# Attention and ReGLU on one core: block 2's scores, values and output copies rearranged amid six output units

## The chip, the cores and the metric

The kernel runs on one core of one Trainium2 chip. The metric is the device time of one execution in microseconds (us). The engines of the core are TensorE (PE: matmuls, with weight loads shown apart as PEld), VectorE (DVE), ScalarE (ACT), GpSimd (POOL) and SyncE (SP). SyncE, ScalarE and GpSimd also issue DMA transfers; in the profile these issues are named SPq, ACTq and POOLq, or appear as DMA_DIRECT2D and DMA_TRANSPOSE.

## The reference

Chunked attention with 8 memory rows in front, then a feed-forward layer with a ReLU gate. Shapes: q, k, v (4, 8, 768, 64), memories (4, 8, 8, 64), gate and value weights (512, 1536), output weights (1536, 512); the output is (3072, 512) in float32.

```python
for c in range(768 // 32):                       # chunks of 32 queries
    c0, c1 = 32 * c, 32 * c + 32
    l0, r1 = max(0, c0 - 16), min(768, c1 + 8)   # keys: 16 to the left, 8 to the right
    k_full = concat([mem_k, k[:, :, l0:r1]], axis=2)
    v_full = concat([mem_v, v[:, :, l0:r1]], axis=2)
    scores = matmul(q[:, :, c0:c1], k_full.T) / 8
    a = exp(scores - max(scores))
    a = a / (sum(a) + 1e-9)
    attn[:, :, c0:c1] = matmul(a, v_full)
x = attn.transpose(0, 2, 1, 3).reshape(3072, 512)
out = (maximum(x @ w_gate, 0) * (x @ w_val)) @ w_out
```

## The kernel before, in words

The 3072 tokens are cut into 8 blocks of 384 (`TB`); a block is half a batch row with all 8 heads. Heads are handled in 4 pairs (`HP`). A block's 384 queries are four windows (`NQ`) of 96, and each window has 128 keys (8 memory rows and a band of 120).

A block's work has two halves. **Attention**, per head pair: `step_s` makes the scores (4 matmuls into `sc_ps`, which has one buffer) and three exponentials on ScalarE (`ex`); `step_v` multiplies `ex` with the values (8 matmuls into `xo_ps` and `xs_ps`, one bank each, whose upper 64 rows are the sums) and takes the logarithm of the sums (`ln`); `step_e` exponentiates to get the reciprocal (`rinv`); `step_m` multiplies both on VectorE into `xT`. **Feed-forward**, in 15 units: 12 gate/value units (`ffn_unit`: 4 gate and 4 value matmuls into two banks, ReLU on ScalarE, product on VectorE) and 3 output units (`out_unit`: 12 matmuls of 512 columns into one bank, copied to `o_sb`, stored). The banks of `g_ps`, `v_ps` and `o_ps` come from one pool of four (`bank`).

The order is written out by hand, and each engine runs its own instructions in that order. Blocks 0 and 1 are opened by a list of steps (`go`). Then `run` weaves the attention of block n into the units of the block ahead of it: `at` says after which unit a head pair's scores come, and `off` how many units later its values come. For block 2 the units are the 12 gate/value units of block 1 and then six output units, three of block 0 and three of block 1. Scores of the four head pairs come after output units 2, 3, 4 and 5, and values half a unit later, in the middle of the next output unit.

From block 2 on, keys and queries reach their layout in four steps: GpSimd's queue loads them (`load_band`, `load_q_tokens`, within `loads`), SyncE issues two DMA transposes (`turn_dma`: `kT`, then `qT`), GpSimd copies the queries apart for the two heads of each pair (`spread_q`, into `qbd`), and TensorE makes the scores. GpSimd runs these in program order: the spread of block 2, the loads of block 3, the spread of block 3, the loads of block 4, and so on.

Of the kernel before, what the change touches and what calls it, by code (L numbers as in the profile page):

```python
# [8 lines left out]
F32 = mybir.dt.float32  # L9
F16 = mybir.dt.float16  # L10
# [7 lines left out]
def kernel(  # L18
# [12 lines left out]
    nc = tc.nc  # L31
# [60 lines left out]
    filler = const.tile([128, 512], F16, name="filler")  # L92
    xo, xs = (xps.tile([128, 512], F32, name=nm)[:, 0:TB] for nm in ("xo_ps", "xs_ps"))
    bias16 = const.tile([128, 3], F16, name="bias16")
    bias1 = const.tile([128, 3], F32, name="bias1")
    perm = const.tile([128, 128], F16, name="perm")
    mln64 = const.tile([128, 1], F32, name="mln64")
    wg = const.tile([128, NFC, DFF], F16, name="wg")
# [130 lines left out]

    def turn_dma(n):  # L230
        kTs[n] = turned.tile([128, NQ, HP, 128], F16, tag="kT", name="kT")
        qTs[n] = turned.tile([128, NQ, HP, QB], F16, tag="qT", name="qT")
        nc.sync.dma_start_transpose(kTs[n].rearrange("p i a m -> p (i a) m"),  # L233
                                    k16s[n % 2].rearrange("p i h d -> p (i h d)"))
        nc.sync.dma_start_transpose(qTs[n].rearrange("p i a m -> p (i a) m"),
                                    q16s[n].rearrange("p i h d -> p (i h d)"))

    def spread_q(n):

        for hh in range(2):  # L240
            s = slice(D * hh, D * hh + D)
            nc.gpsimd.tensor_copy(qbds[n % 2][s, :, :, hh, :].rearrange("p i a m -> p (i a) m"),  # L242
                                  qTs[n][s].rearrange("p i a m -> p (i a) m"))

# [87 lines left out]
    def step_v(n, hp):  # L332
        ex, vw = exs.pop((n, hp)), vwins[n % 2]
        for i in range(NQ):
            for hh in range(2):
                nc.tensor.matmul((xo, xs)[hh][:, QB * i:QB * i + QB], lhsT=vw[:, i, 2 * hp + hh, :],  # L336
                                 rhs=ex[:, hh, i, :], start=True, stop=True)
        ln = rpool.tile([D, 2, TB], F32, name="ln")
        for hh in range(2):
            nc.scalar.activation(ln[:, hh], (xo, xs)[hh][D:128], ACT.Ln, scale=1.0 / 64.0)  # L340
        lns[n, hp] = ln
# [6 lines left out]
    def step_m(n, hp):  # L348
        rinv = rinvs.pop((n, hp))
        for hh in range(2):  # L350
            nc.vector.tensor_tensor(out=x_of(n)[D * hh:D * hh + D, hp, :], in0=(xo, xs)[hh][0:D],  # L351
                                    in1=rinv[:, hh, :], op=ALU.mult)
# [48 lines left out]
    def out_unit(n, t, between=()):  # L401
# [10 lines left out]
        if last:  # L412
            for s, copy, dma in ((slice(0, 256), dve_copy, sp), (slice(256, 512), act_copy, act_dma)):
                copy(o_sb[:, s], o_ps[:, s])
                dma(out[row0:row0 + 128, s], o_sb[:, s])
        else:
            nc.scalar.copy(o_sb, o_ps)  # L417
            act_dma(out[row0:row0 + 128, :], o_sb)
# [226 lines left out]
    load_mem_v(2)  # L645
    turn_dma(2)
    load_band(2, v, vwins)
# [17 lines left out]


    STEP = {"s": step_s, "v": step_v, "e": step_e, "m": step_m}

    def pieces(n, what):
        for w, hp in what:  # L670
            STEP[w](n, hp)

    def run(order, n, at, off, turn_at):
        for u, (b, x) in enumerate(order):
            now = [hp for hp in range(HP) if n < NB and u == at[hp] + off]
            if n < NB:
                pieces(n, [("m", hp) for hp in range(HP) if u == at[hp] + off + 1])
            inner, outer = ("ve", "") if x >= NDC else ("v", "e")  # L680
            unit(b, x, [lambda w=(w, hp): pieces(n, [w]) for hp in now for w in inner])
# [3 lines left out]
            if n == 2 and u < len(clear):  # L685
                clear[u]()
            if u == turn_at and n + 1 < NB:
                turn_dma(n + 1)
                spread_q(n + 1)
        if n < NB:  # L690
            pieces(n, [("m", hp) for hp in range(HP) if len(order) == at[hp] + off + 1])

# [44 lines left out]
```

## Time and profile before

| | us |
|---|---|
| median of 3 runs (lowest, highest) | 245.21 (240.61, 245.4) |
| profiled execution, its own time | 241.14 |
| its span, first to last instruction | 239.1 |

The table of the page in 40 slices of 5.98 us each; each digit is the busy share in tenths:

```profile
PE   7899999999876599999999999999999999999994
DVE  4677548871031245512662155604652166314400
ACT  3473874432577488927984589728892699434321
POOL 8879655623980696199059602990040000000000
PEclk9999999999999999999999999999999999999999
DMA  6999999999999699979959999799901100120012
```

The stretch around the change is slices 9 to 14 (54 to 84 us). In the rows that follow, "idle before" and the square brackets give the idle time of the engine ahead of an instruction and what ended it. Line numbers are those of the kernel before.

### The profile page before, as it was taken

What the parts mean: (1) busy time and instruction counts of PE and PEld (TensorE: products, weight loads), DVE (VectorE), ACT (ScalarE), POOL (GpSimd) and SP (SyncE); (2) the same over time, 40 slices, a digit from 0 to 9 for tenths busy, and PEclk for the clock granted to TensorE, in tenths of its full rate; (3) what the DMA queues carried; (4) which work ended last, traced back from release to release, by engine and by line L of the source; (5) the groups of instructions that cost most, each with busy time, mean ns of one, the idle gap of its engine ahead of it and who ended that gap; (6) DMA issues with size and microseconds to landing.
All of it is one profiled execution on the core that took longest, in us unless ns stands there. A gap on an engine that the chain in (4) does not pass through costs nothing.

```text
span 239.1 us, 4590 instructions
## 1 busy us (share of the span) xinstructions
PE 225.6 (94%) x1727; PEld 130.8 (55%) x1727; DVE 104.8 (44%) x204; ACT 142.7 (60%) x300; POOL 104.2 (44%) x131
## 2 busy tenths in 40 slices
PE   7899999999876599999999999999999999999994
PEld 3556455655433266646664566546664666555541
DVE  4677548871031245512662155604652166314400
ACT  3473874432577488927984589728892699434321
POOL 8879655623980696199059602990040000000000
PEclk9999999999999999999999999999999999999999
DMA  6999999999999699979959999799901100120012
GB/s 164 175 195 196 196 192 206 154 129 128 136 174 185 161 100 151 142 88 187 164 87 90 183 151 102 50 171 132 169 3 61 71 3 0 44 91 0 1 44 88
DMA packets 110143, 28.47 MB, mean 119 GB/s; under 512 B 93882, under 2 KB 107178, under 8 KB 110122
## 3 DMA queue, kind: packets, MB, share of 16 engines
q0 software_dynamic: 81760, 15.13, 79.6%
q1 hardware_dynamic: 24490, 6.50, 19.0%
q10 hardware_dynamic: 3872, 6.56, 8.3%
q8 instruction: 13, 0.21, 0.4%
q14 instruction: 8, 0.07, 0.1%
HBM read 31.08 MB, written 6.29 MB: 156 GB/s over the span
## 4 chain that ended last, share of the span: by engine, by line
PE 67%; DMA 19%; POOL 7%; SPq 2%; issue 2%; DVE 1%; ACT 0%
PE g_ps L372 20%; PE v_ps L372 20%; PE o_ps L408 18%; DMA qT<-q16n 5%; DMA wg<-in_moe_w_gate_dram 5%; DMA k<-in_k_dram 4%; PE sc_ps L279 3%; DMA vwin<-in_v_dram 2%; POOL k L145 2%; SPq L233 2%; POOL qbd L242 2%; DMA kst<-in_k_dram 2%; PE xo_ps L336 1%; PE xs_ps L336 1%; POOL q16n L171 1%
## 5 line engine op out<-in xcount | busy, mean ns | idle before, releaser
L384 DVE TENSOR_TENSOR gv<-v_ps,gr 128x384 f16<-128x384 f32 x95 | 52.5, 555 | 88.7 <-ACT gr L380 72.8
L372 PE MATMUL g_ps<-xT,wg 128*128 128x384 f16 x380 | 78.5, 326 | 1.3 <-DVE xT L351 1.3
L372 PE MATMUL v_ps<-xT,wv 128*128 128x384 f16 x380 | 78.1, 326 | 0.4 <-DMA wv<-in_moe_w_val_dram 0.4
L408 PE MATMUL o_ps<-wo,gv 128*128 128x512 f16 x288 | 64.6, 379 | 0.0
L380 ACT ACTIVATE gr<-g_ps 128x384 f16<-128x384 f32 x95 | 46.3, 488 | 26.1 <-PE g_ps L372 13.5
L372 PEld LDWEIGHTS <-wv 128*128 128x128 f16 x384 | 36.1, 98 | 24.1 <-issue 1.5
L372 PEld LDWEIGHTS <-wg 128*128 128x128 f16 x384 | 36.7, 98 | 22.8 <-issue 0.2
L408 PEld LDWEIGHTS <-gv 128*128 128x128 f16 x288 | 27.9, 98 | 31.3
L242 POOL COPY qbd<-qT 64x1536 f16<-64x1536 f16 x12 | 17.6, 1464 | 58.8 <-DMA qT<-q16n 58.4
L291 ACT ACTIVATE ex<-sc_ps,bias 128x256 f16<-128x256 f32 x84 | 33.4, 469 | 6.8 <-PE sc_ps L255 2.4
L417 ACT COPY o_sb<-o_ps 128x512 f32<-128x512 f32 x23 | 13.5, 586 | 35.1 <-PE o_ps L408 24.9
L351 DVE TENSOR_TENSOR xT<-xo_ps,rinv 64x384 f16<-64x384 f32 x24 | 13.2, 550 | 25.1 <-ACT rinv L345 25.1
L145 POOL DMA_DIRECT2D k<-in_k_dram x24 | 21.5, 905 | 2.9 <-DMA wv<-in_moe_w_val_dram 1.9
L345 ACT ACTIVATE rinv<-ln,mln 64x768 f32<-64x768 f32 x24 | 22.2, 925 | 0.1
L145 POOL DMA_DIRECT2D vwin<-in_v_dram x24 | 21.8, 940 | 0.4 <-PE v_ps L372 0.4
L171 POOL DMA_DIRECT2D q16n<-in_q_dram x24 | 18.7, 798 | 3.4 <-DMA wo<-in_moe_w_out_dram 3.4
L340 ACT ACTIVATE ln<-xo_ps 64x384 f32<-64x384 f32 x24 | 11.7, 487 | 13.7 <-PE xs_ps L336 13.7
L336 PEld LDWEIGHTS <-vwin 128*128 128x128 f16 x192 | 10.9, 98 | 8.6 <-issue 5.5
L336 PE MATMUL xo_ps<-ex,vwin 128*128 128x96 f16 x96 | 11.2, 206 | 4.3 <-ACT ex L291 4.3
L351 DVE TENSOR_TENSOR xT<-xs_ps,rinv 64x384 f16<-64x384 f32 x24 | 13.2, 551 | 0.7
L279 PE MATMUL sc_ps<-qbd,kT 128*128 128x192 f16 x96 | 11.8, 246 | 1.3 <-POOL qbd L242 1.3
L340 ACT ACTIVATE ln<-xs_ps 64x384 f32<-64x384 f32 x24 | 11.4, 474 | 0.0
(89 smaller groups left out, 128.4 us busy)
## 6 DMA issues: line engine op xcount, KB each, us to landing
out_dram<-o_sb ACTq DMA_DIRECT2D x23, 256.0 KB
q16n<-in_q_dram POOLq DMA_DIRECT2D x24, 96.0 KB, 5.3
k<-in_k_dram POOLq DMA_DIRECT2D x18, 120.0 KB, 4.8
vwin<-in_v_dram POOLq DMA_DIRECT2D x18, 120.0 KB, 7.6
wg<-in_moe_w_gate_dram POOLq DMA_DIRECT2D x6, 256.0 KB, 8.4
wv<-in_moe_w_val_dram POOLq DMA_DIRECT2D x6, 256.0 KB, 8.7
wo<-in_moe_w_out_dram POOLq DMA_DIRECT2D x3, 512.0 KB, 11.6
rv<-in_v_dram POOLq DMA_DIRECT2D x4, 224.0 KB, 8.1
```

What stands on the lines that cost most here:

```text
L145: pool_dma(dsts[p][NMEM + m0:NMEM + m1, i, :, 0:D], src)
L171: pool_dma(q16s[n][:, i], src)
L242: nc.gpsimd.tensor_copy(qbds[n % 2][s, :, :, hh, :].rearrange("p i a m -> p (i a) m"), qTs[n][s].rearrange("p i a m -> p (i a) m"))
L291: nc.scalar.activation(flat[:, :, :, s], view[:, :, :, s], ACT.Exp, scale=SCALE, bias=(bias1 if n == 1 else bias)[:, g:g + 1])
L336: nc.tensor.matmul((xo, xs)[hh][:, QB * i:QB * i + QB], lhsT=vw[:, i, 2 * hp + hh, :], rhs=ex[:, hh, i, :], start=True, stop=True)
L340: nc.scalar.activation(ln[:, hh], (xo, xs)[hh][D:128], ACT.Ln, scale=1.0 / 64.0)
L345: nc.scalar.activation(rinv, lns.pop((n, hp)), ACT.Exp, scale=-1.0, bias=mln64[0:D, :])
L351: nc.vector.tensor_tensor(out=x_of(n)[D * hh:D * hh + D, hp, :], in0=(xo, xs)[hh][0:D], in1=rinv[:, hh, :], op=ALU.mult)
L372: nc.tensor.matmul(ps[a], lhsT=(wg, wv)[a][:, f, 128 * m:128 * m + 128], rhs=xTs[n][:, f, :], start=(f == 0), stop=(f == NFC - 1))
L380: nc.scalar.activation(grs[n, m], g_ps, ACT.Relu)
L384: nc.vector.tensor_tensor(out=gvs[n][:, m, :], in0=v_ps, in1=grs.pop((n, m)), op=ALU.mult)
L408: nc.tensor.matmul(o_ps, lhsT=gvs[n][:, m, 128 * t:128 * t + 128], rhs=wo[:, m, :], start=(m == 0), stop=(m == NDC - 1))
```

## The change

Between block 1's gate/value units and block 2's own units, and at the start of block 2's units, the order becomes another one:

- `run1` and `pair2` replace the general `run` for block 2. Scores and exponentials of head pair hp come in the middle of output unit hp+2, and its values one unit later, directly behind the next pair's scores.
- Values of pairs 0 and 2 go to two banks of the pool of four (`xo2_ps`, `xs2_ps`), those of pairs 1 and 3 to `xo_ps` and `xs_ps`.
- `spread_q(2)` runs on VectorE. Every spread is now four copies, the first head pair's two ahead. On GpSimd a copy of one column (`gate`) from `kT` of block 2 stands ahead of the loads of block 3, where the spread stood.
- The six output units are copied by VectorE and stored by SyncE; `o_sb` has 4 buffers in place of 3. The transposes of block 3 come at output units 2 (`kT`) and 3 (`qT`), in program order between these stores, where both stood at unit 4 before.
- Block 2's first two gate/value units are computed together, chunk by chunk (`chunk`), and block 3's scores come after units 1, 4, 7 and 10 in place of 0, 3, 6 and 9.

The diff, cut to its core:

```diff
-    opool = ctx.enter_context(tc.tile_pool(name="opool", bufs=3))
+    opool = ctx.enter_context(tc.tile_pool(name="opool", bufs=4))
...
-    def spread_q(n):
-        for hh in range(2):
-            s = slice(D * hh, D * hh + D)
-            nc.gpsimd.tensor_copy(qbds[n % 2][s, :, :, hh, :].rearrange("p i a m -> p (i a) m"),
-                                  qTs[n][s].rearrange("p i a m -> p (i a) m"))
+    def spread_q(n, copy=nc.gpsimd.tensor_copy):
+        for a in (slice(0, 1), slice(1, HP)):
+            for hh in range(2):
+                s = slice(D * hh, D * hh + D)
+                copy(qbds[n % 2][s, :, a, hh, :], qTs[n][s, :, a, :])
...
     def step_v(n, hp):
         ex, vw = exs.pop((n, hp)), vwins[n % 2]
+        if n == 2 and hp % 2 == 0:
+            xo, xs = (bank(nm)[:, 0:TB] for nm in ("xo2_ps", "xs2_ps"))
+        else:
+            xo, xs = xo_ps, xs_ps
+        vbanks[n, hp] = xo, xs
...
+        elif n < 2:
+            dve_copy(o_sb, o_ps)
+            sp(out[row0:row0 + 128, :], o_sb)
         else:
             nc.scalar.copy(o_sb, o_ps)
             act_dma(out[row0:row0 + 128, :], o_sb)
...
+            if n == 3 and u < 2:
+                if u == 0:
+                    ffn_open(2, (0, 1))
+                    for f in range(NFC):
+                        chunk(2, f)
+                    ffn_close(2)
+            else:
+                unit(n - 1, u, ...)
...
+    def pair2(hp):
+        if hp < HP:
+            score(2, hp)
+        if hp > 0:
+            step_v(2, hp - 1)
+        if hp > 1:
+            step_m(2, hp - 2)
+        if hp < HP:
+            score_exp(2, hp)
+        if hp > 0:
+            step_ln(2, hp - 1)
+            step_e(2, hp - 1)
+
+    def run1():
+        for u in range(NDC):
+            unit(1, u)
+            if u < len(clear):
+                clear[u]()
+        spread_q(2, dve_copy)
+        for t in range(2 * NT):
+            out_unit(t // NT, t % NT, [lambda: pair2(t - 1)] if t > 0 else [])
+            if t == 1:
+                turn_k_dma(3)
+            if t == 2:
+                turn_q_dma(3)
+            if t == 3:
+                spread_q(3)
+        step_m(2, HP - 1)
...
-    spread_q(2)
+    nc.gpsimd.tensor_copy(gate, kTs[2][:, NQ - 1, HP - 1, 0:1])
     loads(3)
-    run([(1, m) for m in range(NDC)] + [(b, NDC + t) for b in range(2) for t in range(NT)], 2, (13, 14, 15, 16), 1, 15)
+    run1()
     for n in range(2, NB):
         loads(n + 2)
-        run([(n, u) for u in range(NDC + NT)], n + 1, (0, 3, 6, 9), 2, 9)
+        run(n + 1, (1, 4, 7, 10) if n == 2 else (0, 3, 6, 9))
```

Three places show how the change moves instructions. ScalarE first, at the output units, in the kernel before (numbers tell buffers apart; `ex` with `x3` are a head pair's exponentials):

```order
L417 COPY o_sb_1085<-o_ps_1072 128x512
L418 DMA out_0_dram<-o_sb_1085 128x512
L417 COPY o_sb_1101<-o_ps_1088 128x512
L418 DMA out_0_dram<-o_sb_1101 128x512
L291 ACTIVATE ex_1109<-sc_ps_1104,bias_103 128x8x32 x3
L340 ACTIVATE ln_1128<-xo_ps_107 64x384
L340 ACTIVATE ln_1128<-xs_ps_108 64x384
L345 ACTIVATE rinv_1131<-ln_1128,mln64_112 64x768
L417 COPY o_sb_1139<-o_ps_1113 128x512
L418 DMA out_0_dram<-o_sb_1139 128x512
L291 ACTIVATE ex_1147<-sc_ps_1142,bias_103 128x8x32 x3
L340 ACTIVATE ln_1169<-xo_ps_107 64x384
```

And in the changed kernel:

```order
L294 ACTIVATE ex_1104<-sc_ps_1099,bias_103 128x8x32 x3
L294 ACTIVATE ex_1141<-sc_ps_1126,bias_103 128x8x32 x3
L350 ACTIVATE ln_1145<-xo2_ps_1131 64x384
L350 ACTIVATE ln_1145<-xs2_ps_1132 64x384
L355 ACTIVATE rinv_1148<-ln_1145,mln64_113 64x768
L294 ACTIVATE ex_1184<-sc_ps_1168,bias_103 128x8x32 x3
L350 ACTIVATE ln_1188<-xo_ps_107 64x384
L350 ACTIVATE ln_1188<-xs_ps_108 64x384
L355 ACTIVATE rinv_1191<-ln_1188,mln64_113 64x768
```

The copies and stores of the output units are gone from between the steps, and the exponentials of pair 1 stand ahead of pair 0's logarithms.

GpSimd, from the spread of block 2 (`qbd0_96`) to the spread of block 3 (`qbd1_97`), before:

```order
L242 COPY qbd0_96<-qT_578 64x16x96 x2
L145 DMA k161_93<-in_k_dram 120x8x64 x3
L145 DMA k161_93<-in_k_dram 112x8x64
L171 DMA q16n_892<-in_q_dram 96x8x64 x4
L145 DMA vwin1_95<-in_v_dram 120x8x64 x3
L145 DMA vwin1_95<-in_v_dram 112x8x64
L242 COPY qbd1_97<-qT_1193 64x16x96 x2
```

And in the changed kernel:

```order
L752 COPY gate_112<-kT_578 128x1
L146 DMA k161_93<-in_k_dram 120x8x64 x3
L146 DMA k161_93<-in_k_dram 112x8x64
L172 DMA q16n_892<-in_q_dram 96x8x64 x4
L146 DMA vwin1_95<-in_v_dram 120x8x64 x3
L146 DMA vwin1_95<-in_v_dram 112x8x64
L246 COPY qbd1_97<-qT_1159 64x4x96 x2
L246 COPY qbd1_97<-qT_1159 64x4x3x96 x2
```

The two copies of `qT` ahead of block 3's loads have become one copy of a column of `kT`.

SyncE's queue, from the memory rows of block 3 (`k161_93`, `vwin1_95`) to those of block 4 (`k160_92`, `vwin0_94`), before:

```order
L156 DMA k161_93<-memk_98 8x4x512
L161 DMA vwin1_95<-memv_99 8x8x64 x4
L233 DMA_TRANSPOSE kT_1192<-k161_93 128x16x128
L235 DMA_TRANSPOSE qT_1193<-q16n_892 128x16x96
L156 DMA k160_92<-memk_98 8x4x512
L161 DMA vwin0_94<-memv_99 8x8x64 x4
```

And in the changed kernel:

```order
L157 DMA k161_93<-memk_98 8x4x512
L162 DMA vwin1_95<-memv_99 8x8x64 x4
L428 DMA out_0_dram<-o_sb_1089 128x512
L428 DMA out_0_dram<-o_sb_1114 128x512
L233 DMA_TRANSPOSE kT_1117<-k161_93 128x16x128
L428 DMA out_0_dram<-o_sb_1156 128x512
L238 DMA_TRANSPOSE qT_1159<-q16n_892 128x16x96
L428 DMA out_0_dram<-o_sb_1199 128x512
L428 DMA out_0_dram<-o_sb_1245 128x512
L428 DMA out_0_dram<-o_sb_1276 128x512
L157 DMA k160_92<-memk_98 8x4x512
L162 DMA vwin0_94<-memv_99 8x8x64 x4
```

Two output stores now precede the K transpose of block 3, one stands between the two transposes, and three follow.

More of the change, by code (lines that the diff above doesn't have):

```diff
@@ L92 @@
     filler = const.tile([128, 512], F16, name="filler")
-    xo, xs = (xps.tile([128, 512], F32, name=nm)[:, 0:TB] for nm in ("xo_ps", "xs_ps"))
+    xo, xs = xo_ps, xs_ps = [xps.tile([128, 512], F32, name=nm)[:, 0:TB] for nm in ("xo_ps", "xs_ps")]
     bias16 = const.tile([128, 3], F16, name="bias16")
@@ L96 @@
     perm = const.tile([128, 128], F16, name="perm")
+    gate = const.tile([128, 1], F16, name="gate")
     mln64 = const.tile([128, 1], F32, name="mln64")
@@ L337, in step_v, with step_ln @@
                                  rhs=ex[:, hh, i, :], start=True, stop=True)
+    def step_ln(n, hp):
         ln = rpool.tile([D, 2, TB], F32, name="ln")
         for hh in range(2):
-            nc.scalar.activation(ln[:, hh], (xo, xs)[hh][D:128], ACT.Ln, scale=1.0 / 64.0)
+            nc.scalar.activation(ln[:, hh], vbanks[n, hp][hh][D:128], ACT.Ln, scale=1.0 / 64.0)
         lns[n, hp] = ln
@@ L350, in step_m @@
         for hh in range(2):
-            nc.vector.tensor_tensor(out=x_of(n)[D * hh:D * hh + D, hp, :], in0=(xo, xs)[hh][0:D],
+            nc.vector.tensor_tensor(out=x_of(n)[D * hh:D * hh + D, hp, :], in0=vbanks[n, hp][hh][0:D],
                                     in1=rinv[:, hh, :], op=ALU.mult)
@@ L645 @@
     load_mem_v(2)
-    turn_dma(2)
+    turn_k_dma(2)
+    turn_q_dma(2)
     load_band(2, v, vwins)
@@ L671, in pieces, with run @@
             STEP[w](n, hp)
-    def run(order, n, at, off, turn_at):
-        for u, (b, x) in enumerate(order):
-            now = [hp for hp in range(HP) if n < NB and u == at[hp] + off]
+    def run(n, at):
+        for u in range(NDC + NT):
             if n < NB:
-                pieces(n, [("m", hp) for hp in range(HP) if u == at[hp] + off + 1])
-            inner, outer = ("ve", "") if x >= NDC else ("v", "e")
-            unit(b, x, [lambda w=(w, hp): pieces(n, [w]) for hp in now for w in inner])
+                pieces(n, [("m", hp) for hp in range(HP) if u == at[hp] + 3])
+            now = [hp for hp in range(HP) if n < NB and u == at[hp] + 2]
+            inner, outer = ("ve", "") if u >= NDC else ("v", "e")
+            if n == 3 and u < 2:
[5 more added lines that the diff above has]
+            else:
+                unit(n - 1, u, [lambda w=(w, hp): pieces(n, [w]) for hp in now for w in inner])
             pieces(n, [(w, hp) for hp in now for w in outer])
@@ L684, in run @@
                 pieces(n, [("s", hp) for hp in range(HP) if u == at[hp]])
-            if n == 2 and u < len(clear):
-                clear[u]()
[L687 to L691, printed above, removed]
+            if u == 9 and n + 1 < NB:
+                turn_k_dma(n + 1)
+                turn_q_dma(n + 1)
+                spread_q(n + 1)
+    def pair2(hp):
[14 more added lines that the diff above has]
+            if u < len(clear):
+                clear[u]()
+        spread_q(2, dve_copy)
[8 more added lines that the diff above has]
+        step_m(2, HP - 1)
     def loads(n):
```

7 lines of the change are left out of this document (4 added, 3 removed).

## The prediction

> **What bounds the kernel now.** I read the page first: busy time by engine, then the chain that ended last.
>
> ```profile
> PE 225.6 (94%) x1727; PEld 130.8 (55%) x1727; DVE 104.8 (44%) x204; ACT 142.7 (60%) x300; POOL 104.2 (44%) x131
> PE 67%; DMA 19%; POOL 7%; SPq 2%; issue 2%; DVE 1%; ACT 0%
> ```
>
> TensorE is busy for 94% of the span, and the chain is TensorE for 67% of it. Nothing off TensorE can be worth more than the gaps in TensorE's work, so the next view is who TensorE waited for. Three of its rows fall in the stretch that the change rewrites:
>
> ```profile
> PE xo_ps L336 <- ACT ex L291: 4.3, 4, 1.2
> PE sc_ps L279 <- POOL qbd L242: 1.3, 1, 1.3
> PE g_ps L372 <- DVE xT L351: 1.3, 1, 1.3
> ```
>
> (Total us, times, longest.) The timeline of TensorE puts them in place:
>
> ```profile
> 55.56 5.34 PE L408 MATMUL o_ps<-wo,gv 128*128 128x512 f16 x24
> 60.74 0.49 PE L279 MATMUL sc_ps<-qbd,kT 128*128 128x192 f16 x4
> 61.07 1.46 PE L408 MATMUL o_ps<-wo,gv 128*128 128x512 f16 x6
> 63.29 0.20 PE L336 MATMUL xo_ps<-ex,vwin 128*128 128x96 f16 x1 [0.76 <-ACT ex L291]
> ...
> 68.05 0.20 PE L336 MATMUL xo_ps<-ex,vwin 128*128 128x96 f16 x1 [1.19 <-ACT ex L291]
> ...
> 68.38 1.46 PE L408 MATMUL o_ps<-wo,gv 128*128 128x512 f16 x6
> ...
> 78.90 0.65 PE L372 MATMUL g_ps<-xT,wg 128*128 128x384 f16 x3
> 80.81 0.32 PE L372 MATMUL g_ps<-xT,wg 128*128 128x384 f16 x1 [1.26 <-DVE xT L351]
> 80.98 0.81 PE L372 MATMUL v_ps<-xT,wv 128*128 128x384 f16 x4
> 83.05 0.49 PE L279 MATMUL sc_ps<-qbd,kT 128*128 128x192 f16 x4 [1.26 <-POOL qbd L242]
> ```
>
> The six output units run from 55.56 to 78.90, with block 2's scores and values between them; block 2's first gate/value unit follows, then block 3's first scores. The cadences: 24 output matmuls from 55.56 to 60.74, so 0.216 each, 1.30 per half unit, 2.59 per unit; a score step 0.33 (60.74 to 61.07); a value step 0.33 (68.05 to 68.38); a gate matmul 0.165 (80.81 to 80.98). A wait costs 0.16 more than its bracket, because a group's modelled end reaches 0.16 past the next start (six output matmuls: 1.46 shown, 1.30 of cadence). The losses are thus 4.3 + 4 x 0.16 = **4.97** (values wait for exponentials), 1.26 + 0.16 = **1.42** (last head pair of xT) and **1.42** (block 3's spread queries): 7.81 us. After 83.05 the list has no TensorE wait.
>
> **Part 1: scores earlier, values on two bank pairs (4.97).** Before, a half output unit, 1.30 us, lies between scores and values. ScalarE in that time:
>
> ```profile
> 62.03 1.21 ACT L291 ACTIVATE ex<-sc_ps,bias 128x256 f16<-128x256 f32 x3 [0.50 <-ACT o_sb L417]
> 63.93 0.49 ACT L340 ACTIVATE ln<-xo_ps 64x384 f32<-64x384 f32 x1 [0.69 <-PE xs_ps L336]
> 64.32 0.47 ACT L340 ACTIVATE ln<-xs_ps 64x384 f32<-64x384 f32 x1
> 64.83 0.94 ACT L345 ACTIVATE rinv<-ln,mln 64x768 f32<-64x768 f32 x1
> 65.79 0.59 ACT L417 COPY o_sb<-o_ps 128x512 f32<-128x512 f32 x1
> 66.41 0.34 ACTq L418 DMA_DIRECT2D out_dram<-o_sb  x1
> ```
>
> The copy and the store's issue (0.59 + 0.34) stand ahead of the exponentials (1.21). After the change a whole unit plus the next scores lies between scores and their values, 2.59 + 0.33 = 2.92 us, and ScalarE does only 1.21 + 0.86 + 0.94 = 3.01 us a step, against TensorE's 2.59 + 0.33 + 0.33 = 3.25. ScalarE keeps pace with 0.24 to spare, the exponentials stand first in each step, and the second bank pair lets values start before VectorE has read the last ones. I book all 4.97. Late next would be VectorE: two multiplies and an output copy a step. Its nearest rows for what is new:
>
> ```profile
> L414 DVE COPY o_sb<-o_ps 128x256 f32<-128x256 f32 x1 | 0.4, 425 | 7.1 <-DMA out_dram<-o_sb 7.1
> L532 DVE CAST rk<-kst 114x512 f16<-114x512 f32 x2 | 1.2, 594 | 2.1 <-DMA kst<-in_mem_k_dram 1.2 <-DMA kst<-in_k_dram 0.9
> L242 POOL COPY qbd<-qT 64x1536 f16<-64x1536 f16 x12 | 17.6, 1464 | 58.8 <-DMA qT<-q16n 58.4
> ```
>
> An output copy of 512 is between 0.43 and twice that, 0.85; I take 0.69, the two copies less one fixed start. With two multiplies of 0.55 that is 1.8 of 3.25: hidden.
>
> New start times on TensorE: units at 55.56, 58.15, 61.07, 64.33, 67.58, 70.83 (2.92 for the one with scores alone, 3.25 or 3.26 for the next three), the last (values only) ending at 73.75; block 2's first gate/value matmuls then start 5.15 earlier than 78.90 (the first value step ran 0.15 longer than the rest; I leave that out).
>
> **Part 2: the spread moves to VectorE.** The first scores now come at 58.15 + 1.30 = 59.45, before at 60.74. The queries land at 57.65:
>
> ```profile
> 47.55 4.79 SPq L233
> ...
> 52.53 5.12 DMA qT<-q16n
> 57.71 1.46 POOL qbd L242
> ```
>
> Two copies of 384 elements must come first. Each lies between 0.2 (the 512-element cast scaled by a third) and 0.59 (that cast itself), so the first pair is ready at 58.1 to 58.9: no wait. By the Trainium skill, "VectorE: DVE Perf Modes", section "Side-by-side: where the cycles go for N=2048 bf16", a 16-bit copy at four elements a cycle would be an estimated 0.27 for 384; the sum would be the same. All four copies take 1.3 to 3.6, so VectorE is free at 59.0 to 61.3, and the first output copy waits there; its bank is wanted again at 62.7, covered.
>
> **Part 3: xT (1.42) and the paired units.** The last values end at 72.5; ln 0.86, exponent 0.94, multiplies 1.10 and handovers of 0.1 to 0.2 each give xT at about 75.8. Gate and value of two units now alternate per chunk, so 12 matmuls (2.0 us from 73.75) come before the last head pair is needed, not 3. New there: the fourth matmul takes the bank of the last output unit, which VectorE has copied at 73.75 + 0.16 + 0.69 = 74.6; TensorE wants it at 74.25, a wait of **0.4**. The thirteenth then comes at 76.1, after xT. I book 1.42 gone, 0.4 added. Scores of block 3 are reached at 73.75 + 2.64 + 0.4 = 76.8.
>
> **Part 4: loads, transposes, SyncE.** These decide the 1.42 of block 3's queries.
>
> ```profile
> 60.63 3.54 POOL L145 DMA_DIRECT2D k<-in_k_dram  x4
> 68.45 4.63 SPq L233 DMA_TRANSPOSE kT<-k  x1
> 73.26 1.90 SPq L235 DMA_TRANSPOSE qT<-q16n  x1
> 78.77 3.50 SPq L161 DMA_DIRECT2D vwin<-memv  x4
> SPq L161 <- DMA kT<-k: 2.8, 1, 2.8
> 73.26 6.70 DMA qT<-q16n
> 80.01 1.46 POOL qbd L242
> ```
>
> Now GpSimd's loads of block 3 wait for both spread copies and start at 60.63; after, they wait for kT alone. When kT(2) lands no row says. It lies between 52.3 (issue end, 47.55 + 4.79) and 57.65. For block 3 SyncE's row at 78.77 had waited 2.8 for kT, which so landed 1.2 ahead of qT (73.26 + 6.70 = 79.96); by that nearest row I take 57.65 - 1.2 = 56.4, so loads start at about 56.5, 4.1 sooner. The K transpose then moves from 68.45 to 64.3. The two output stores now ahead of it on SyncE are copied by 61.8 to 62.7 (the second unit ends at 61.07; VectorE is free by 61.3 at the latest, then two copies), so they do not hold it; a third stands between it and the Q transpose and adds an issue of about 0.4, hidden behind the K transpose's own issue of 4.63. Transpose start to landing was 79.96 - 68.45 = 11.5, so queries land at 75.8 to 76.2 (the store's 256 KB included). GpSimd copies the first head pair alone, two of 384 elements: 0.37 each by proportion, 0.73 at twice that; I take 0.45, ready at 77.1 against 76.8. Wait **0.3 to 0.5**, taken as 0.5; bounds are none (kT(2) at the early end) and 4.0 (below). Block 3's scores stand one unit later, which is why 76.8 suffices. The other three stores go behind; the fifth buffer use needs only the first store, long landed. The final blocks keep their order; the next block's queries have 4 us of slack.
>
> **Sum:** -4.97 - 1.42 - 1.42 + 0.4 + 0.5 = -6.9. The profiled execution took 241.14 (span 239.1 and 2.04 around it): **234.2**. That execution lies 4.1 below the median of the runs shown, 245.21, and 0.5 above the lowest; my number stands to the changed kernel's times as this profile to those.
>
> **Rivals.**
>
> *Block 3's queries land late (0.20).* Transposes vary in this trace:
>
> ```profile
> 157.75 5.20 SPq L233 DMA_TRANSPOSE kT<-k  x1
> 173.46 2.99 POOL L242 COPY qbd<-qT 64x1536 f16<-64x1536 f16 x2 [12.49 <-DMA qT<-q16n]
> ```
>
> That pair took 15.7, against 10.2 and 11.6 for blocks 2 and 3; late there costs nothing. With 15.7 from 64.3, queries are ready at 80.9, a wait of 4.1 instead of 0.5: 237.8. For: loads now overlap the end of block 2's transposes. Against: the distance from loads to transposes is unchanged.
>
> *VectorE's copies starve the loads (0.08).* The spread copies (1.3 to 3.6 us) now run while GpSimd issues loads. A similar overlap exists before:
>
> ```profile
> 45.58 3.61 POOL L145 DMA_DIRECT2D vwin<-in_v_dram  x4 [0.42 <-PE v_ps L372]
> 46.15 0.91 DVE L496 MEMSET vwin<- 128x1024 uint32 x1 [0.16 <-issue]
> 67.21 3.61 POOL L145 DMA_DIRECT2D vwin<-in_v_dram  x4
> ```
>
> Four issues took 3.61 with VectorE writing and 3.61 without, but a memset reads nothing. If copies did block, loads and all behind them slip by 1.3 to 3.6: 235.5 to 237.8. The Trainium skill, "SBUF — State Buffer", section "Who interferes with whom", states this rule: a two-port VectorE copy locks GpSimd out, descriptor writing included. By that rule this rival holds; no run here shows it.
>
> *The value waits stay in part (0.08).* ScalarE's step took 62.03 to 65.77 = 3.74 by the clock, its wait of 0.69 included. If that span, not 3.01, sets the pace, four steps lose 0.5 each: 236.2.
>
> *Slower than before (0.04).* Both transpose pairs take 15.7. Block 2's queries land at 47.55 + 15.7 = 63.25, scores wait for VectorE until 64.0 (4.5 added); the output copies queue behind the spread on VectorE, SyncE's K transpose behind their stores, until about 68.3; block 3's queries are ready at 84.9 where TensorE stands at 81.3 (3.6 added instead of 0.5). 234.2 + 4.5 + 3.1 = 241.8. It decides once the two waits together pass 6.9 + 0.5.
>
> **Numbers.** Forecast 234.2 with 0.60 (233.3 to 235.6). The range runs from 232.8 (no new wait, 233.3, and the lowest run's 0.5 below the profiled one) to 238.8 (late queries, 237.8, and 1 us for stores in between); it leaves out under 0.1. Over 2%, about what a measurement of this kernel tells from no change, means below 236.3: the forecast, the low half of the starving, most of the pace case: 0.70. Within 2%: late queries and the rest, 0.28. Slower by over 2%: 0.02, the last rival with transposes longer still.
>
> **What would show it.** The wait of values for exponentials gone; TensorE's six units some 18.2 us long, not 23.3; the gate copy on GpSimd near 56.4, K transpose near 64.3; one wait on qbd under 1 us at about 76.8. Wrong if qbd waits exceed 2 us, if the first scores wait for VectorE, or if the exponentials still end the value waits.

## The result, and the profile after

The changed kernel takes **235.84 us** (median of 12 executions, 233.51 to 238.66); the kernel before, on the same chip, 244.71 (15 executions, 240.61 to 246.41). The ratio is **0.9717**, 95% interval 0.9668 to 0.9766: faster. Forecast was 234.2 (232.8 to 238.8). The ratio is taken over executions at most 1.5% above the fastest of their kernel, and as those of the kernel before spread over 3%, which of them count shifts from one group of runs to the next (here the medians alone would give 0.964). Kernels of different groups are therefore set against each other by their medians.

One thing about the kernel before is needed to read these numbers. Of its 46 executions beside the experiments, 8 had a mean granted clock of 0.998 to 1.000 and took 240.06 to 242.02; the other 38 had 0.984 to 0.993 and took 243.12 to 247.92. The execution profiled before the prediction (241.14, clock 1.000) was one of the first kind; experiment 1 shows the second. The profiled execution of the changed kernel is the longest of its 12, so its lines show where time can go, and the experiments what the median has of it.

The page of the changed kernel: busy times, the clock, the chain that ended last.

```profile
PE 226.6 (96%) x1727; PEld 131.3 (55%) x1727; DVE 110.8 (47%) x214; ACT 139.1 (59%) x294; POOL 103.5 (44%) x140
PEclk9999999999999799999999999999999999999999
PE 65%; DMA 25%; POOL 5%; SPq 3%; issue 1%; DVE 0%; ACT 0%; POOLq 0%
```

TensorE is busy for as long as before; the span went from 239.1 to 236.8 in these two executions. DMA has grown in the chain from 19% to 25%, and the clock dips in slice 14 (77 to 83 us). Of the three waits shown before, one is left, and a small one is new (total us, times, longest):

```profile
PE sc_ps L282 <- POOL qbd L246: 3.4, 1, 3.4
PE v_ps L382 <- DVE o_sb L427: 0.3, 1, 0.3
```

Waits of values for exponentials and of gate matmuls for xT are gone. TensorE's timeline in the same execution:

```profile
55.14 4.05 PE L418 MATMUL o_ps<-wo,gv 128*128 128x512 f16 x18
59.02 0.49 PE L282 MATMUL sc_ps<-qbd,kT 128*128 128x192 f16 x4
...
73.36 0.33 PE L382 MATMUL g_ps<-xT,wg 128*128 128x384 f16 x1
...
74.30 0.32 PE L382 MATMUL v_ps<-xT,wv 128*128 128x384 f16 x1 [0.29 <-DVE o_sb L427]
...
76.25 0.33 PE L382 MATMUL v_ps<-xT,wv 128*128 128x384 f16 x1
79.93 0.49 PE L282 MATMUL sc_ps<-qbd,kT 128*128 128x192 f16 x4 [3.36 <-POOL qbd L246]
80.26 1.32 PE L382 MATMUL g_ps<-xT,wg 128*128 128x384 f16 x4
81.38 1.48 PE L382 MATMUL v_ps<-xT,wv 128*128 128x384 f16 x4
82.66 1.39 PE L382 MATMUL g_ps<-xT,wg 128*128 128x384 f16 x4
83.89 0.21 PE L344 MATMUL xo_ps<-ex,vwin 128*128 128x96 f16 x1
```

The six output units run from 55.14 to 73.36, 18.2 us against 23.3 before. Then comes the loss: block 3's scores, reached at 76.4, start at 79.93. And behind the gap twelve gate/value matmuls take 80.26 to 83.89, 3.63 us, 0.30 each where 0.163 is their cadence. Windows of the gap and of what follows (us, busy time by engine, then the granted clock, DMA share, GB/s):

```profile
73.36:79.93 6.57, 2.92 (x17) 1.55 (x16) 2.72 (x5) 1.56 (x3) 1.00 (x2) 1.00 1.66 258
79.93:84.39 4.46, 4.46 (x25) 2.48 (x25) 0.56 (x1) 1.65 (x5) 4.40 (x5) 0.62 0.22 31
```

The clock is 1.00 up to the scores and 0.62 behind them. SyncE's queue, GpSimd and VectorE of the same execution show where the queries' time went:

```profile
60.32 1.60 SPq L428 DMA_DIRECT2D out_dram<-o_sb  x2
64.27 5.83 SPq L233 DMA_TRANSPOSE kT<-k  x1
70.15 0.57 SPq L428 DMA_DIRECT2D out_dram<-o_sb  x1
70.91 2.87 SPq L238 DMA_TRANSPOSE qT<-q16n  x1
73.88 2.07 SPq L428 DMA_DIRECT2D out_dram<-o_sb  x3
```

```profile
55.98 0.19 POOL L752 COPY gate<-kT 128x1 f16<-128x1 f16 x1 [7.32 <-DMA kT<-k]
56.47 3.68 POOL L146 DMA_DIRECT2D k<-in_k_dram  x4 [0.30 <-issue]
78.82 3.46 POOL L246 COPY qbd<-qT 64x384 f16<-64x384 f16 x4 [12.03 <-DMA qT<-q16n]
```

```profile
57.47 2.10 DVE L246 COPY qbd<-qT 64x384 f16<-64x384 f16 x4 [1.50 <-DMA qT<-q16n]
```

The gate let the loads go at 56.47 and the K transpose was issued at 64.27, both as forecast. But from there to the spread of block 3 passed 78.82 - 64.27 = 14.55 us. This stretch, **K transpose issued to spread begun**, is called the transpose stretch below; it was 11.56 in the profile before (68.45 to 80.01).

### The profile page after: what moved, and what is told of

The parts are those of the page before. It is cut to its first block, busy times and chain, and to the rows that moved or that the text cites. A ratio compares the mean times of both kernels' runs of the same rounds, so it can differ in the third digit from the quotient of the medians.

```text
span 236.8 us, 4594 instructions
## 1 busy us (share of the span) xinstructions
PE 226.6 (96%) x1727; PEld 131.3 (55%) x1727; DVE 110.8 (47%) x214; ACT 139.1 (59%) x294; POOL 103.5 (44%) x140
## 4 chain that ended last, share of the span: by engine, by line
PE 65%; DMA 25%; POOL 5%; SPq 3%; issue 1%; DVE 0%; ACT 0%; POOLq 0%
PE o_ps L418 20%; PE g_ps L382 20%; PE v_ps L382 19%; DMA wv<-in_moe_w_val_dram 8%; DMA k<-in_k_dram 6%; DMA kT<-k 4%; DMA qT<-q16n 3%; DMA wg<-in_moe_w_gate_dram 3%; PE sc_ps L282 3%; SPq L233 3%; POOL k L146 2%; PE xs_ps L344 1%; PE xo_ps L344 1%; POOL rv L499 1%; POOL qbd L246 0%
## 5 line engine op out<-in xcount | busy, mean ns | idle before, releaser
L382 PE MATMUL g_ps<-xT,wg 128*128 128x384 f16 x380 | 80.4, 330 | 0.0
L382 PE MATMUL v_ps<-xT,wv 128*128 128x384 f16 x380 | 79.8, 328 | 0.3 <-DVE o_sb L427 0.3
L418 PE MATMUL o_ps<-wo,gv 128*128 128x512 f16 x288 | 64.3, 379 | 0.0
L390 ACT ACTIVATE gr<-g_ps 128x384 f16<-128x384 f32 x95 | 46.1, 488 | 27.2 <-PE g_ps L382 14.6
L246 POOL COPY qbd<-qT 64x384 f16<-64x384 f16 (+1 forms) x20 | 16.5, 823 | 52.3 <-DMA qT<-q16n 51.5
L430 ACT COPY o_sb<-o_ps 128x512 f32<-128x512 f32 x17 | 10.0, 586 | 28.6 <-PE o_ps L418 18.6
L350 ACT ACTIVATE ln<-xo_ps 64x384 f32<-64x384 f32 x24 | 11.7, 487 | 14.0 <-PE xs_ps L344 13.9
L361 DVE TENSOR_TENSOR xT<-xo_ps,rinv 64x384 f16<-64x384 f32 x24 | 13.2, 549 | 9.7 <-ACT rinv L355 9.7
L361 DVE TENSOR_TENSOR xT<-xs_ps,rinv 64x384 f16<-64x384 f32 x24 | 13.2, 551 | 0.7
L282 PEld LDWEIGHTS <-kT 128*128 128x128 f16 x96 | 8.7, 98 | 7.1 <-issue 3.5
L344 PEld LDWEIGHTS <-vwin 128*128 128x128 f16 x192 | 10.8, 98 | 3.1 <-issue 0.2
```

Source lines behind the costliest of these rows:

```text
L246: copy(qbds[n % 2][s, :, a, hh, :], qTs[n][s, :, a, :])
L282: nc.tensor.matmul(sc[:, i // 2, 192 * (i % 2):192 * (i % 2) + 192], lhsT=kTs[n][:, i, hp, :], rhs=qbds[n % 2][:, i, hp].rearrange("p h m ...
L350: nc.scalar.activation(ln[:, hh], vbanks[n, hp][hh][D:128], ACT.Ln, scale=1.0 / 64.0)
L382: nc.tensor.matmul(ps[a], lhsT=(wg, wv)[a][:, f, 128 * m:128 * m + 128], rhs=xTs[n][:, f, :], start=(f == 0), stop=(f == NFC - 1))
L390: nc.scalar.activation(grs[n, m], g_ps, ACT.Relu)
L418: nc.tensor.matmul(o_ps, lhsT=gvs[n][:, m, 128 * t:128 * t + 128], rhs=wo[:, m, :], start=(m == 0), stop=(m == NDC - 1))
```

## The experiments

Ratios are to the kernel before on the same chip, its median there 244.4 to 244.7, with 95% intervals.

### 1. The kernel before again

No edit; the question is what its common execution looks like.

> The kernel before, unchanged, for another profile: its median in these comparisons is 244.5, and the execution profiled first took 241.14. Theory D (stores that ScalarE issues during block 3's transposes stretch them): issue to spread of block 3 takes 14 to 16 us in an execution near 244.5, against 11.6 in the one of 241.14, and the wait of block 3's scores for the queries is 4 to 5 us in place of 1.3. Rival W (the weight loads of the first 50 us differ): that wait is 1.3 again, and the output units start 3 us later than 55.56.

Its profiled execution took 247.41 (median of its eight executions 243.85; ratio 0.9974, 0.9898 to 1.0051; one execution of 298.18 had a mean clock of 0.758, and no profile shows why). The wait, the queue behind it, and the window that follows the gap:

```profile
68.61 4.37 SPq L233 DMA_TRANSPOSE kT<-k  x1
84.15 2.98 POOL L242 COPY qbd<-qT 64x1536 f16<-64x1536 f16 x2 [12.17 <-DMA qT<-q16n]
87.19 0.80 PE L279 MATMUL sc_ps<-qbd,kT 128*128 128x192 f16 x4 [5.00 <-POOL qbd L242]
87.19:91.00 3.81, 3.81 (x15) 2.03 (x15) 0.35 (x1) 1.69 (x4) 3.81 (x5) 0.50 0.91 57
```

The K transpose goes out at the same time as in the first profile (68.45), but its stretch is 15.54, so the wait is 5.00 instead of 1.26, and the clock behind it 0.50. Twelve gate/value matmuls at that clock take 3.83 (87.78 to 91.61) instead of 1.95, the scores 0.59 instead of 0.33: 2.1 us. 3.74 + 2.1 is 5.8 of the 6.27 by which this execution is longer than the first. So the profile that the forecast rested on is the rarer, short case. This one is near the long end (of the 46 executions the longest took 247.92); that the other common ones lose a part of the same is likely from their clocks, but only these two executions were profiled.

### 2. Part 1 alone

In the kernel before, scores in the middle of output units, values a unit later on two bank pairs; copies, stores, spread and transposes stay where they were.

```diff
-    run([(1, m) for m in range(NDC)] + [(b, NDC + t) ...], 2, (13, 14, 15, 16), 1, 15)
+    def run1():
...
+        for t in range(2 * NT):
+            out_unit(t // NT, t % NT, [lambda: pair2(t - 1)] if t > 0 else [])
+            if t == 3:
+                turn_dma(3)
+                spread_q(3)
+    run1()
```

> The kernel before with one part of the change: block 2's scores in the middle of output units 2 to 5, values a whole unit later on two bank pairs. Theory C (a chain of loads and transposes sets when block 3's scores can start; TensorE's savings ahead of it are lost there unless the chain is shortened too): value waits (4.97 us) mostly gone, but the wait of block 3's scores for the spread queries grows from 1.4 to 5 to 7 us, time within 1 us of before, or up to 2 us slower if the granted clock falls after so long a gap. Rival A (the terms add): 4 to 5 us faster, wait on the queries unchanged at 1.4.

Measured 246.63, ratio 1.0086 (1.0045 to 1.0128). All waits for exponentials are gone, and yet the time has not fallen. The wait that took their place, then ScalarE and GpSimd:

```profile
PE g_ps L379 <- DVE xT L358: 7.8, 1, 7.8
```

```profile
76.09 0.58 ACT L424 COPY o_sb<-o_ps 128x512 f32<-128x512 f32 x1
81.92 0.34 ACTq L425 DMA_DIRECT2D out_dram<-o_sb  x1
82.36 0.49 ACT L347 ACTIVATE ln<-xo_ps 64x384 f32<-64x384 f32 x1 [5.68 <-DMA qT<-q16n]
81.90 2.98 POOL L242 COPY qbd<-qT 64x1536 f16<-64x1536 f16 x2 [10.45 <-DMA qT<-q16n]
```

ScalarE has copied the fifth output unit by 76.67 and issues its store only at 81.92, when block 3's queries have landed; the logarithms of the last head pair queue behind it. The profile names that landing as what ended the 5.68 us; a store needs nothing of the queries, and why this one waited for them the trace does not show. So the landing of block 3's queries ended the gap, as one theory had it, but at xT by way of ScalarE's queue, which none had.

### 3. Gate, spread and loads alone

```diff
-    spread_q(2)
+    nc.gpsimd.tensor_copy(gate, kTs[2][:, NQ - 1, HP - 1, 0:1])
     loads(3)
...
+            if n == 2 and u == NDC:
+                spread_q(2, dve_copy)
```

(with the four-copy `spread_q`), on the kernel before.

> The kernel before with the other part: loads of block 3 behind a copy of one column of kT, block 2's spread in four copies on VectorE; output copies and stores stay on ScalarE. Theory C: loads start near 56.4 in place of 60.6, block 3's queries land 3 to 4 us sooner, the wait of 1.4 on them goes and the value waits stay: 1.2 to 1.6 us faster, no more. Rival V (loads that overlap the transposes stretch them): the transposes of block 3 take 14 us or more from issue to landing in place of 11.5, part of the wait stays: 0 to 1 us faster. Rival A: 1.4 us faster.

240.07, ratio 0.9811 (0.978 to 0.9843): 4.4 under the median before. The waits for `ex` (4.3) and xT (1.3) stand as before; that for `qbd` is gone, with a transpose stretch of 14.4 (65.87 to 80.24). By the first profile this edit could bring 1.4 at most, and 1.6 was the most expected. Against the long execution of experiment 1 it also saves the longer wait and the half clock behind it, which fits the clocks: 0.998 or more in all five executions, where most of the kernel before have 0.993 or less.

### 4. Block 3's scores one unit later

```diff
-        run(n + 1, (1, 4, 7, 10) if n == 2 else (0, 3, 6, 9))
+        run(n + 1, (2, 5, 8, 11) if n == 2 else (0, 3, 6, 9))
```

in the changed kernel.

> The changed kernel with block 3's scores after units 2, 5, 8 and 11 in place of 1, 4, 7 and 10. Theory C: one more unit (1.3 us) covers the wait on block 3's queries (3.4 in the profile of the changed kernel): the wait falls to about 2 there, or to nothing where the transposes are quicker, and the time by 1.0 to 1.3 us, by 2 to 3 us in executions in which the granted clock fell after the wait. Rival A (that wait is peculiar to the profiled execution and other executions had none): time unchanged within 0.3 us.

234.35, ratio 0.9592 (0.9561 to 0.9624), 1.5 under the changed kernel. No wait on `qbd` is left; its chain in SyncE's queue and GpSimd:

```profile
65.39 4.50 SPq L233 DMA_TRANSPOSE kT<-k  x1
77.67 3.46 POOL L246 COPY qbd<-qT 64x384 f16<-64x384 f16 x4 [9.85 <-DMA qT<-q16n]
```

A stretch of 12.28 here. So late queries cost the changed kernel about 1.5 us in the median.

### 5. Block 2's first units apart

```diff
-            if n == 3 and u < 2:
+            if False:
```

> The changed kernel with block 2's first two gate/value units one after the other as before, not together. Theory C: TensorE waits some 1.4 us for the last head pair of xT again, but reaches block 3's scores that much later, so that the wait on the queries shrinks as much: time unchanged within 0.4 us. Rival A: 1.0 to 1.4 us slower.

235.06 (234.65 to 236.31), ratio 0.962 (0.9585 to 0.9654): no slower than the changed kernel, whose executions lie on both sides of it. Two waits of 1.3 (xT) and 0.3 (`qbd`) take the place of one on `qbd`. A wait on xT ahead of block 3's scores takes the place of one at them, so doing the units in pairs brings nothing here.

### 6. The chain undone

The changed kernel with block 2's spread on GpSimd ahead of the loads again, and no gate.

```diff
-        spread_q(2, dve_copy)
...
-    nc.gpsimd.tensor_copy(gate, kTs[2][:, NQ - 1, HP - 1, 0:1])
+    spread_q(2)
     loads(3)
```

> The changed kernel with block 2's spread back on GpSimd ahead of block 3's loads (no gate copy, nothing spread on VectorE); output copies stay on VectorE and stores on SyncE. Theory C: loads of block 3 start near 60 to 61 in place of 56, its queries land 4 to 5 us later, and TensorE waits that much longer ahead of block 3's scores; the first scores of block 2 wait up to 1 us as well; 239 to 242, with more where the gap brings the granted clock down. Rival A (terms add): only the 1.4 us of the wait on queries comes back: 237.

239.65, ratio 0.9887 (0.9815 to 0.996): 3.8 over the changed kernel. The K transpose goes out at 68.83, 4.6 later. Its stretch is only 10.9, and still:

```profile
PE sc_ps L282 <- POOL qbd L246: 3.9, 1, 3.9
80.82:84.50 3.68, 3.68 (x15) 1.93 (x15) 0.56 (x1) 1.69 (x4) 3.62 (x4) 0.55 0.12 28
```

Here too the clock, 0.55, follows the gap. 3.8 of the 8.9 us between the medians thus hang on the chain's start.

### 7. The gate on the queries

```diff
-    nc.gpsimd.tensor_copy(gate, kTs[2][:, NQ - 1, HP - 1, 0:1])
+    nc.gpsimd.tensor_copy(gate, qTs[2][:, NQ - 1, HP - 1, 0:1])
```

> The changed kernel with the gate copy reading the last column of qT in place of kT, so that block 3's loads start when block 2's queries have landed, some 1.5 us later. Theory C: all behind it moves by 1.5, and the wait of block 3's scores grows by 1.0 to 1.5: 236.8 to 237.5. Rival V (loads that overlap the Q transpose stretch transposes): block 2's queries land sooner and block 3's transposes take less than 12 us, time unchanged within 0.5.

236.75, ratio 0.9759 (0.9686 to 0.9832), 0.9 over the changed kernel, with executions (235.63 to 241.02) that overlap its own. The gate comes at 57.77, the K transpose at 67.01, its stretch is 10.8. The longest wait is 2.29, and behind it the clock stays whole:

```profile
78.88:83.00 4.12, 4.12 (x34) 2.76 (x34) 0.56 (x1) 2.90 (x8) 4.05 (x5) 1.00 0.17 38
```

A later start was given back in part by a shorter stretch. That loads and transposes disturb each other less in this order would explain it; one profile does not show it.

### 8. No gate

The gate's line is deleted, so loads of block 3 start without waiting for block 2's transposes.

> The changed kernel without the gate copy: block 3's loads are issued right behind those of block 2, some 7 us sooner, beside both transposes of block 2. Theory C with rival V in it: block 2's queries land 2 to 5 us later and its first scores wait for VectorE by 1 to 4 us; block 3's queries land sooner, so the wait on them goes; time between 234 and 238. Without any contention: block 2 unchanged, no waits left, 233.5 to 234.5.

238.72, ratio 0.9837 (0.977 to 0.9905), 2.9 over the changed kernel (one of its six executions took 336.88 at a mean clock of 0.658; without it the median is 238.70). The wait has moved to block 2, whose spread on VectorE starts when its queries land:

```profile
PE sc_ps L282 <- DVE qbd L246: 2.6, 1, 2.6
62.20 1.51 DVE L246 COPY qbd<-qT 64x384 f16<-64x384 f16 x4 [5.11 <-DMA qT<-q16n]
```

The spread starts at 62.20 in place of 57.47, and block 2's scores wait until 62.89; block 3's do not wait, with a stretch of 9.6 (66.00 to 75.61). So the gate is worth its place: earlier loads make the block 2 transposes late.

### 9. Stores issued by ScalarE

The changed kernel, where ScalarE issues the six stores that VectorE has copied.

```diff
             dve_copy(o_sb, o_ps)
-            sp(out[row0:row0 + 128, :], o_sb)
+            act_dma(out[row0:row0 + 128, :], o_sb)
```

> The changed kernel with the six stores issued by ScalarE in place of SyncE (copies stay on VectorE). Theory C: ScalarE has 0.35 us more a step, 3.4 against TensorE's 3.25, with over 1 us of slack ahead of the values: no value waits; without stores between them the two transposes of block 3 start 0.5 to 0.8 us closer, and its queries land up to 1 us sooner: 0 to 1 us faster. Rival S (the stores in SyncE's queue are what stretches the transposes from 11.6 to 12 to 14.5 us): issue to spread back at 11.6 or less, 1 to 2 us faster. Rival P: ScalarE's pace shows, waits of values for exponentials return: 1 us slower.

242.97, ratio 1.0035 (0.999 to 1.008). Who issues six stores decides 7.1 us, most of the 8.9 between the medians of the two kernels; none of the three expectations had this. No value waits: ScalarE keeps pace. SyncE's queue, ScalarE's stores, GpSimd and TensorE, with the window behind the gap:

```profile
64.19 5.15 SPq L233 DMA_TRANSPOSE kT<-k  x1
69.51 5.43 SPq L238 DMA_TRANSPOSE qT<-q16n  x1
...
64.94 0.34 ACTq L428 DMA_DIRECT2D out_dram<-o_sb  x1
68.20 0.34 ACTq L428 DMA_DIRECT2D out_dram<-o_sb  x1
71.47 0.34 ACTq L428 DMA_DIRECT2D out_dram<-o_sb  x1
...
74.39 0.34 ACTq L428 DMA_DIRECT2D out_dram<-o_sb  x1
...
82.46 3.46 POOL L246 COPY qbd<-qT 64x384 f16<-64x384 f16 x4 [15.75 <-DMA qT<-q16n]
83.58 0.80 PE L282 MATMUL sc_ps<-qbd,kT 128*128 128x192 f16 x4 [6.89 <-POOL qbd L246]
83.58:87.50 3.92, 3.92 (x15) 2.19 (x15) 0.46 (x1) 1.70 (x4) 3.86 (x4) 0.50 0.06 11
```

The K transpose starts at 64.19, the Q transpose even earlier than in the changed kernel (69.51 against 70.91), and the stretch is 18.3 us. Four stores go out while the transposes are being issued (64.19 to 74.94), where SyncE's queue puts one between them and holds three back until both are issued.

### 10. SyncE's stores alone

The kernel before, ScalarE still copying, but SyncE storing the six units, with `kT` turned after output unit 2, `qT` after unit 3, and four buffers for `o_sb`.

```diff
-            act_dma(out[row0:row0 + 128, :], o_sb)
+            (sp if n < 2 else act_dma)(out[row0:row0 + 128, :], o_sb)
...
+            if n == 2 and u == NDC + 1:
+                turn_k_dma(3)
+            if n == 2 and u == NDC + 2:
+                turn_q_dma(3)
```

> The kernel before with the six stores of the output units issued by SyncE in place of ScalarE, block 3's K transpose behind two of them and its Q transpose behind a third, as in the changed kernel; four buffers for o_sb; copies stay on ScalarE. Theory D: block 3's transposes take 11.5 to 12.5 us from issue to spread in most executions, the wait on its queries falls by 2 to 4, value waits by 0.3 each (no store issue ahead of the exponentials): 240 to 242. Rival S0 (the queue of a store makes no difference to the transposes, 0.4 us as the prediction had it): 243 to 244.5, from the value waits alone.

241.9, ratio 0.9882 (0.9808 to 0.9956), 2.7 under the median before. The K transpose goes out at 69.62, 1.2 later than before, its stretch is 10.9, and block 3's scores wait 2.2. The waits for exponentials have shrunk as well:

```profile
PE sc_ps L285 <- DMA vwin<-memv: 2.2, 1, 2.2
PE xo_ps L342 <- ACT ex L297: 2.0, 3, 0.7
```

(The first line names a DMA; the spread on GpSimd ends at 83.51, just ahead of the scores at 83.57.) Without the store's issue on ScalarE the values wait 0.67 a time in place of 1.19, 2.0 in all against 4.3 in the first profile. That alone is about what the edit gains, so this run does not show that the transposes gained from it.

### 11. No stores

The six stores left out of the changed kernel.

```diff
             dve_copy(o_sb, o_ps)
-            sp(out[row0:row0 + 128, :], o_sb)
```

> The changed kernel without the six stores (the output rows of blocks 0 and 1 are left out). Theory D: with no store in SyncE's queue or beside the transposes, block 3's transposes take 10.5 to 12 us from issue to spread, queries are ready at about the 76.4 at which TensorE gets there, wait under 1 us: 233.5 to 235. Rival S0: 12 to 14.5 us as before, 235 to 236.

234.34 (four executions), ratio 0.9626 (0.9547 to 0.9704); stretch 11.7, no `qbd` wait. The output rows of blocks 0 and 1 are not written here. Without any store the kernel gains 1.5 us, as much as experiment 4 gains by asking later: SyncE's stores are not free, and cost at most that.

### 12. One unit later, queries next to keys

Experiment 4, and `qT` turned right behind `kT`.

```diff
                 turn_k_dma(3)
-            if t == 2:
                 turn_q_dma(3)
```

> The changed kernel with block 3's scores one unit later (as in the run that did so) and the Q transpose issued right behind the K transpose, the third store behind both. Theory C and D: queries land 0.5 to 1.5 us sooner than with the store between; no wait of block 3's scores in any execution; 233.5 to 234.4, equal to or 0.5 us below the run with scores one unit later alone. Rival: the store between costs nothing that is left: equal within 0.3.

234.35, ratio 0.961 (0.9566 to 0.9654), executions 233.95 to 234.52; stretch 13.2, a `qbd` wait of 0.8. No difference from experiment 4. The queries were expected 0.5 to 1.5 us sooner; with no store between the transposes the stretch is not shorter (12.3 there). These two are the best versions: 4% under the kernel before.

### The runs together

| | median, us | less the median before | stretch, us | wait of block 3's scores, us |
|---|---|---|---|---|
| before, first profile | (241.14) | | 11.6 | 1.26 |
| before, again | 243.85 | | 15.5 | 5.00 |
| part 1 alone | 246.63 | +2.2 | 12.4 | (xT) 7.80 |
| gate, spread, loads alone | 240.07 | -4.4 | 14.4 | none |
| SyncE's stores alone | 241.9 | -2.7 | 10.9 | 2.2 |
| the change | 235.84 | -8.9 | 14.6 | 3.36 |
| chain undone | 239.65 | -5.0 | 10.9 | 3.87 |
| stores by ScalarE | 242.97 | -1.6 | 18.3 | 6.89 |
| scores one unit later | 234.35 | -10.1 | 12.3 | none |
| units apart | 235.06 | -9.4 | 12.1 | 0.25 |
| gate on the queries | 236.75 | -7.9 | 10.8 | 2.29 |
| no gate | 238.72 | -5.9 | 9.6 | none (block 2: 2.58) |
| one later, queries next to keys | 234.35 | -10.3 | 13.2 | 0.80 |
| no stores | 234.34 | -10.3 | 11.7 | none |

(Stretch and wait are those of the one profiled execution.) Three parts alone, +2.2, -4.4 and -2.7, make -4.9; the change gives -8.9. The 4.0 between them can't be put down to the parts helping each other: VectorE's copies of the output units and block 3's scores after unit 1 in place of 0 belong to the change and were not run alone. What is shown is that part 1 costs time alone, although its 4.97 us of waits are gone: it is worth nothing until the stores and the queries are out of its way. The parts share one chain: keys of block 2 land, gate, loads of block 3, K transpose, Q transpose, spread, scores of block 3. What TensorE saves ahead of these scores counts only as far as that chain ends sooner too.

## Why the prediction was right, and where it was wrong

The time is 1.6 above the forecast and inside the range. Step by step:

- **Values waiting for exponentials (4.97 gone): right.** Six units in 18.22 us, forecast 18.2; the wait is absent. But in experiment 2, with ScalarE's store held up and the queries as late as before, the same saving brought nothing: the sum treated it as a saving of its own.
- **xT gone, bank wait of 0.4: right.** No xT wait; 0.29 + 0.16 on the bank. By experiment 5 the xT term and the `qbd` term are alternatives rather than a sum.
- **Gate and K transpose: right.** 55.98 and 64.27, forecast 56.4 and 64.3, in an execution whose output units start 0.42 earlier. The loads of k took 3.68 for four issues, while VectorE's spread ran, against 3.54 before: the rival that VectorE starves them cost 0.14 at most here. VectorE paid more itself: its first two copies took 0.43 each beside the loads, and 0.25 in experiment 7, where the loads start just behind them, at 58.26.
- **Queries of block 3 (wait 0.5): the step that failed.** The stretch was taken as 11.5 from one profiled execution; with SyncE's stores it measured 9.6 to 14.6 in the changed kernel and its variants. The profiled wait is 3.36 + 0.16, and the half clock behind it 3.63 - 1.95 = 1.68. Together with the 0.42 these turn the forecast's 234.2 into 234.2 + 3.02 + 1.68 - 0.42 = 238.5, against 238.66 measured for that execution. By the prediction's own words ("wrong if qbd waits exceed 2 us") it was wrong here, and this is the rival called late queries, at its price of a 4.1 us wait less 0.6. In the median the loss is 1.5, by experiments 4, 11 and 12, so the common case lies between forecast and rival.
- **Stores on SyncE (one issue of about 0.4, taken as hidden, with its 256 KB in the transposes' time): mis-sized.** Placed on SyncE they cost at most 1.5 (experiment 11); left with ScalarE they would have cost 7.1 more (experiment 9). The prediction priced the issue of a moved store and, in its upper bound alone, 1 us for stores between the transposes; it did not ask what stores in ScalarE's queue would do to the transposes. This is the largest difference that one edit makes in the study.
- **Base.** The sum was made against an execution with clock 1.000. From it the gain is 241.14 - 235.84 = 5.3, against 6.9 forecast; from median to median it is 8.9. The half clock that follows a long gap, about 2 us a time, was in no term, because the one profile that was read did not have it. The prediction also said that 234.2 would stand to the changed kernel's times as the profile to those of the kernel before, 4.1 under the median; it came 1.6 under. From the median of 244.71 the same sum would have given 237.8, 2.0 too long, because the common execution before loses more at block 3's queries than the sum took away. That the short execution as base came nearer is luck.

What stays open: why the stretch varies between 11.6 and 15.5 in the same kernel (profile and experiment 1), and how much of the 18.3 is the separate queue and how much the moment of the stores. A run with ScalarE's stores at SyncE's moments was not made, and the stretches, one profile each, overlap: 11.6 to 18.3 with ScalarE's stores, 9.6 to 14.6 with SyncE's. Nor is the stretch only a matter of crowded transfers. In the changed kernel's profile the DMA engines moved 31 GB/s from 68.0 to 70.0 us, amid the K transpose's issue, against 177 GB/s in the 3.7 us before and 145 in the 4.0 after; what held them up there is not known. The Trainium skill, "DMA: Bandwidth & Descriptors", section "Queues, rings and completion order", says that a DMA engine takes turns packet by packet between the queues that have work, and works through one queue's ring in order; a stretch of 18.3 with stores in a queue of their own would fit that, but no run separates it from the moment of the stores. The Trainium skill, same page, section "Issuing engines are not separate DMA queues", says that issuing from several engines saves no more than sequencer time. It doesn't say what it can cost: between experiment 9 and the change 7.1 us hang on the issuer.

## What to carry to other kernels

Before summing waits on one engine, find the transfer chain that the last of them hangs on: a saving ahead of it is a loan until that chain ends sooner. Price a moved store by what it does to the transfers that others wait for, on the old queue and on the new one, and where a transfer's length has been read once, read it again in another execution before a term rests on it. If a late transfer can't be sped up, ask for it later: asking one unit later for block 3's scores was worth 1.5 us.

## What the runs showed of the hardware that was not expected

**The clock follows the gap.** TensorE gaps of 3.36, 3.87, 5.00 and 6.89 us were followed by a granted clock of 0.62, 0.55, 0.50 and 0.50 over the next 3.7 to 4.5 us; behind gaps of 2.29 and 2.58 it was 1.00. A late transfer is thus paid twice, once as the wait and then as some 1.7 to 2.1 us of slow matmuls. The Trainium skill, "TensorE: Matmul & The Clock Gate", section "What's actually happening", has the clock halved after an idle window of about 3.4 us and restored after about as much sustained work; these rows agree, and a wait that falls now short of it and now beyond it would explain the two kinds of executions of the kernel before (two of them were profiled: a wait of 1.26 with clock 1.000, one of 5.00 with 0.986).

**A store can wait for a foreign transpose.** ScalarE's fifth store in experiment 2 went out 5.25 us after its copy had ended, when the queries landed (81.92 - 76.67), and everything behind it on ScalarE waited too.
